# Attention scores with each head's high and low products in one half of the array's rows

## The chip, the cores and the metric

One core of a Trainium2 chip runs the whole kernel as one launch. The metric is the device time of that launch in microseconds (us). The engines are TensorE (PE; its weight loads are listed as PEld), VectorE (DVE), ScalarE (ACT), GpSimd (POOL) and SyncE (SP), which here issues nearly all DMAs from one queue in order.

## What is computed

Three layers in a row. The change touches the first alone: attention for 4 batches of 12 heads, 448 tokens and 64 values per head.

```python
q_n, k_n = (rmsnorm(q, g_q), rmsnorm(k, g_k))
scores = scale * np.matmul(q_n, k_n.transpose(0, 1, 3, 2))
scores = scores - np.max(scores, axis=-1, keepdims=True)
attn = np.exp(scores)
attn = attn / (np.sum(attn, axis=-1, keepdims=True) + 1e-09)
return np.matmul(attn, v)
```

Then every token goes to one of eight experts with places for 224 tokens each (an ordered, greedy choice), through `relu(x @ w1) @ w2`, and then through `(h * cos(h)) @ w_out` with `h = x @ w_in`.

## The kernel before, in words

The 48 heads are worked through as 24 pairs. Attention and the two later layers are two separate plans. Within a plan every operation is recorded as a step with a cost estimate (`Plan.cost`), and `Plan.run` then places all steps by list scheduling on its own estimates; the order in which each engine gets its instructions is fixed by that, and at run time each engine works its list off in order. All recorded operations have the line of the recording helper (L47) in the profile; the DMAs inside the kernel that copy between partitions have L363 (`copy`), and warm-up matmuls L385.

For a pair, `front` loads q and k, squares and normalises; `turn` scales a normalised tile `qn`, transposes it on TensorE (`t`), and splits it into a high part rounded to the fast matmul type F32R (`hi`, an ACT step) and the rest (`lo`, a DVE step). In these 128-partition tiles the pair's first head has partitions 0 to 63 and its second 64 to 127. The scores then want high times high, high times low and low times high. To fill the array's 128 rows for one head, `turn` rearranges by DMA: `TK` has the head's high keys twice (side by side) and its low keys in the other 64 partitions, `QS` the high queries twice and the low queries. These are four DMAs a head (two for keys, two for queries).

`shifts` takes an upper estimate per query of the row's scores: seven matmuls into two PSUM banks (`s`), each followed by a DVE maximum over the bank (`cm`); the result is transposed and negated (`cr`) and copied by DMA into partition 64 of `QS`, beside a row of ones in `TK`. `scores` does, for each of 4 chunks of 112 keys and each head, two matmuls of 448 columns into one PSUM bank (`st`): one over 128 rows (high times high and low times high), one over 65 rows (high times low, and the shift). ACT takes the exponential into `pf`. There are two `st` banks, so one head's exponential runs beside the other head's matmuls. `weigh` multiplies with v (`po`: 64 output columns, both heads in the two halves of the array's columns) and sums (`dn`: four groups of 32 columns), `rows` and `tail` normalise and turn back (`dn` with `wg`, `t`), and x goes to DRAM.

In the main loop pair P's scores, the shifts of P+1, the turn of P+3, the load of P+6 and the end of P-1 are recorded together. The first three pairs are worked ahead of it; for pair 0 a special `shift` does each head alone, the first of them over 64 rows. The plan also holds 56 of the 96 steps of `Narrow`, which converts w_in and w_out (a DMA in, ACT and DVE work, a DMA out: `nr`, `na`), and 150 warm-up matmuls; both are fillers of low urgency.

Of the kernel before, what the change touches and what calls it, by code (L numbers as in the profile page):

```python
# [50 lines left out]
class Plan:  # L51
# [4 lines left out]
    def __init__(self, nc):  # L56
        self.nc, self.steps, self.seen, self.group, self.rush = nc, [], {}, None, 0.0
        self.shared, self.ahead, self.beside = True, 0.0, False
        self.tensor = Engine(self, "PE", nc.tensor)
        self.vector = Engine(self, "DVE", nc.vector)  # L60
        self.scalar = Engine(self, "ACT", nc.scalar)
        self.gpsimd = Engine(self, "POOL", nc.gpsimd)

    def cost(self, eng, name, out, r, kw):
        n = max([out.free_size()] + [x.free_size() for x in r])
        if eng == "PE":
            if self.key(out)[1]:
                return 0.055
            rhs = r[1] if name == "matmul" else r[0]
            passes = 1 if rhs.dtype != F32 else 4 if name == "matmul" else 2  # L70
            if name == "matmul" and rhs.dtype == F32 and self.beside:
                passes *= {32: 0.32, 64: 0.6}.get(out.partition_size(), 1)
            return max(out.free_size() / 2333.0 + 0.011, 0.107 if rhs.dtype == F32R else 0.0467) * passes
# [217 lines left out]
NHL = 3  # L291
# [15 lines left out]
def attention(tc, P, R, ident, q, k, v, g_q, g_k, w_gate, x_dram, L, other):  # L307
# [4 lines left out]
    with ExitStack() as ctx:  # L312
# [8 lines left out]
        TK = [cst.tile([128, 2, S], F32R, name=f"tk{i}") for i in range(8)]  # L321
        QS = [cst.tile([128, 2, 2, S], F32R, name=f"qs{i}") for i in range(4)]
# [12 lines left out]
        hls = ring("hl", NHL, [128, 2, S], F32R)  # L335
        his = ring("kh", 4, [128, S], F32R)
        los = ring("kl", 2, [128, S], F32R)
# [59 lines left out]
        for t in TK:  # L397
            zset(t[D:D + 1, 1], 1.0)
# [31 lines left out]
        def turn(P_, i, rs, j):  # L430

            if True:
                qn = qns()
                x = first[P_][:, i].rearrange("p h (c d) -> p h c d", d=D)
                r = rs[:, i, j:j + 2].unsqueeze(3).to_broadcast([CP, 2, NC, D])
                mul = P.vector.tensor_tensor if P_ < UP else P.gpsimd.tensor_tensor
                mul(qn.rearrange("p c (h d) -> p h c d", h=2), x, r, op=ALU.mult)
                p = bt()
                P.begin()
                for c in range(NC):  # L440
                    pe.transpose(p[:, c * CP:(c + 1) * CP], qn[:, c], ident[0:CP, 0:CP])
                P.finish()
                if i:
                    hi, lo = keys[P_], _ = his(), los()
                else:
                    hl = hls()
                    hi, lo = hl[:, 0], hl[:, 1]
                if P_ == 0:
                    o = TK[0][0:D, 0] if i else QS[0][0:D, 0, 0]
                    sc.activation(o, p[0:D, :S], AF.Copy, scale=gs[0:D] if i else 1.0)  # L450
                if i:
                    sc.activation(hi, p[:, :S], AF.Copy, scale=gs)
                    ve.scalar_tensor_tensor(lo, p[:, :S], gs, hi.bitcast(F32), op0=ALU.mult, op1=ALU.subtract)
                else:
                    sc.activation(hi, p[:, :S], AF.Copy)
                    ve.tensor_tensor(lo, p[:, :S], hi.bitcast(F32), op=ALU.subtract)
                for h in range(2):
                    r = slice(h * D, (h + 1) * D)
                    if P_ == 0 and h == 0:
                        if i:  # L460
                            copy(TK[0][0:D, 1], hi[r])
                            copy(TK[0][D:128, 0], lo[r])
                        else:
                            copy(QS[0][D:128, 0, 0], hl[r, 0])
                            copy(QS[0][0:D, 1, 0], hl[r, 1])
                    elif i:
                        t = TK[(2 * P_ + h) % 8]
                        copy(t[0:D], hi[r].unsqueeze(1).to_broadcast([D, 2, S]))
                        copy(t[D:128, 0], lo[r])
                    else:  # L470
                        t = QS[P_ % 4]
                        copy(t[D:128, 0, h], hl[r, 0])
                        copy(t[0:D, :, h], hl[r])
                    if P_ and not i:
                        z = slice(S - D, S) if h == 0 else slice(0, D)
                        P.either("tensor_copy", mix[P_ % 4][r, r], hi[r, z])

        keys = {}

        def shifts(P_):  # L480


            cm, t, x = cms(), QS[P_ % 4], 7
            for m in range(x):
                p = b1()[:, :S]
                if m == 3:
                    w, y = mix[P_ % 4], keys.pop(P_)
                else:
                    h, c = (0, 128 * m) if m < 3 else (1, D + 128 * (m - 4))
                    w, y = t[:, 0, h, c:c + 128], TK[(2 * P_ + h) % 8][:, 0]  # L490
                pe.matmul(p, w, y, start=True, stop=True)
                ve.tensor_reduce(cm[:, m:m + 1], p, AX.X, ALU.max)
# [3 lines left out]
            copy(t[D:D + 1, 1].rearrange("o j s -> o (j s)").rearrange("o (m p) -> o m p", p=128), cr)  # L496

        def shift(P_, heads=(0, 1)):

            cm, t = cms()[0:CP], QS[P_ % 4]  # L500
            K = D if P_ == 0 and heads[0] == 0 else 128
            for h in heads:
                for c in range(NC):
                    p = b1()[0:CP, :S]
                    pe.matmul(p, t[0:K, 0, h, c * CP:(c + 1) * CP], TK[(2 * P_ + h) % 8][0:K, 0], start=True, stop=True)
                    ve.tensor_reduce(cm[:, h * NC + c:h * NC + c + 1], p, AX.X, ALU.max)
            n, o = len(heads) * NC, heads[0] * NC
            p = bt()[0:n, 0:CP]
            pe.transpose(p, cm[:, o:o + n], ident[0:CP, 0:CP])
            cr = crs()[0:n, 0:CP]  # L510
            sc.activation(cr, p, AF.Copy, scale=-1.0)
            row = t[D:D + 1, 1, heads[0]:heads[-1] + 1]
            copy(row.rearrange("o j (c p) -> o (j c) p", c=NC), cr)
# [17 lines left out]
        def scores(P_, a, z):  # L531

            qs = QS[P_ % 4]
            for c in range(a, z):
                sl = slice(c * CP, (c + 1) * CP)
                for h in range(2):
                    p, tk = bs()[0:CP, :S], TK[(2 * P_ + h) % 8]

                    def both():
                        pe.matmul(p, tk[:, 0, sl], qs[:, 0, h], start=True, stop=False)  # L540
                        pe.matmul(p, tk[0:D + 1, 1, sl], qs[0:D + 1, 1, h], start=False, stop=True)

                    block(both)
                    pf = exps[P_, h, c] = pfs()
                    sc.activation(pf[0:CP], p, AF.Exp)
# [116 lines left out]
        for P_ in range(min(NPR, AHEAD)):  # L662
# [4 lines left out]
            if P_ == 0:  # L667
                shift(0, (0,))
                shift(0, (1,))
# [689 lines left out]
```

## Time and profile before

| | |
|---|---|
| median of three runs | 1274.76 us (1274.62 to 1276.87) |
| the profiled execution | 1281.06 us, its span 1279.0 us |
| TensorE matmul busy | 1191.9 us (93%) |
| TensorE weight load busy | 955.5 us (75%) |
| VectorE busy | 889.9 us (70%) |
| ScalarE busy | 673.6 us (53%) |
| mean granted clock of TensorE | 0.956 of 2.4 GHz |

Attention lies in the first 385 us of the span: the first `st` matmul starts at 25.9 us and the last at 376.6. The shares of the table are means over attention, the routing (some 385 to 420 us) and the experts, so the argument below reads from attention's own stretches. In "the chain of waits" each piece is the work that the next piece waited for, with its start, its length and how many instructions are merged in it; the pieces of an engine that is never waiting follow one another, so their lengths add up to the time.

### The profile page before, as it was taken

The page shows a single profiled execution, that of the slowest core. Times are in us where ns is not written, and L with a number is a line of the kernel's source. Part 1 is how long each engine was busy: PE and PEld are TensorE (multiplying, and loading weights), DVE is VectorE, ACT ScalarE, POOL GpSimd, SP SyncE. Part 2 cuts the span into 40 slices and gives each one's busy share as a digit, 9 for nine tenths or more (in the row PEclk, how much of TensorE's full clock was granted, in tenths as well). Part 3 has the DMA queues.
Part 4 walks back from the last instruction along what each step waited for, and adds up shares of the span by engine and source line. Part 5 has one row for each costly group of instructions (what it writes and reads, how often), then busy time and mean ns, then how long its engine had stood idle before and what let it go on. Part 6 is the DMA issues. An engine that isn't in the chain of part 4 may idle for free.

```text
span 1279.0 us, 21567 instructions
## 1 busy us (share of the span) xinstructions
PE 1191.9 (93%) x7247; PEld 955.5 (75%) x7247; DVE 889.9 (70%) x2710; ACT 673.6 (53%) x1655; POOL 99.9 (8%) x156
## 2 busy tenths in 40 slices
PE   7999999999894999999979999899999989999996
PEld 5455455544442898878869988789998878999996
DVE  6768888798769888898487569457648737646501
ACT  5677666675553545763364458254538434535400
POOL 5211111021000000000001000000100000100001
PEclk9999998999995899999989999999999999999998
DMA  9787999886853578879956776855775783766762
GB/s 216 168 202 214 230 250 241 239 240 200 229 168 116 164 220 289 288 265 308 279 174 186 219 225 218 242 197 156 228 217 203 237 254 114 224 202 218 240 203 71
DMA packets 207953, 273.56 MB, mean 214 GB/s; under 512 B 17474, under 2 KB 178531, under 8 KB 201699
## 3 DMA queue, kind: packets, MB, share of 16 engines
q1 hardware_dynamic: 205282, 261.18, 69.3%
q0 software_dynamic: 2560, 11.01, 3.0%
q8 instruction: 57, 0.93, 0.3%
q14 instruction: 54, 0.43, 0.1%
HBM read 202.79 MB, written 36.46 MB: 187 GB/s over the span
## 4 chain that ended last, share of the span: by engine, by line
PE 60%; DMA 16%; DVE 16%; ACT 2%; SPq 2%; issue 2%; POOL 0%; POOLq 0%; DVEq 0%; ACTq 0%
PE acc L47 37%; PE st L47 5%; PE po L47 5%; PE dn L47 4%; PE t L47 3%; PE s L47 3%; DMA AB<-rows 3%; DVE r L47 2%; DMA w_out<-nr 2%; DMA nr<-in_moe_w_out_dram 2%; DVE oh L47 2%; DMA wx<-w_out 2%; DVE AB L47 2%; DVE na L47 1%; PE rt L47 1%
## 5 line engine op out<-in xcount | busy, mean ns | idle before, releaser
L47 PE MATMUL acc<-gh,wx 128*128 128x224 f32 (+1 forms) x1952 | 375.0, 316 | 5.4 <-DMA wx<-w_out 3.6
L47 PEld LDWEIGHTS acc<-gh,wx 128*128 128x128 f32 x1952 | 285.3, 194 | 27.7 <-issue 8.8
L47 PE MATMUL acc<-x2h,wx 128*128 128x448 f32 x768 | 229.9, 375 | 0.0
L47 DVE TENSOR_TENSOR wx<-ws,wx 128x768 fp32r<-128x768 f32 (+1 forms) x112 | 119.9, 1070 | 62.0 <-ACT wx L1179 61.9
L47 PEld LDWEIGHTS acc<-x2h,wx 128*128 128x128 f32 x768 | 147.1, 192 | 19.0 <-issue 6.5
L1179 ACT ACTIVATE wx<-ws 128x768 fp32r<-128x768 f32 (+1 forms) x110 | 103.0, 937 | 101.7 <-PE acc L47 71.0
L47 PE MATMUL acc<-gl,wx 128*128 128x448 f32 (+1 forms) x400 | 146.8, 367 | 0.8 <-DVE gl L47 0.8
L47 PE MATMUL acc<-x2l,wx 128*128 128x448 f32 x384 | 142.5, 371 | 0.0
L47 PE MATMUL acc<-xe,wx 128*128 128x224 f32 x1152 | 138.0, 281 | 1.0 <-DVE xe L47 0.7
L47 PEld LDWEIGHTS acc<-xe,wx 128*128 128x128 f32 x1152 | 135.4, 197 | 1.6 <-DVE xe L47 0.9
L47 DVE TENSOR_REDUCE cm<-s 128x1 f32<-128x448 f32 (+1 forms) x169 | 100.1, 616 | 36.7 <-PE s L47 35.9
L47 ACT ACTIVATE pf<-st 112x448 f32<-112x448 f32 x192 | 95.7, 539 | 45.2 <-PE st L47 42.6
L47 ACT ACTIVATE oh<-oh 128x896 bf16<-128x896 bf16 x80 | 75.3, 942 | 74.9 <-DVE oh L47 74.6
L47 PE MATMUL st<-qs,tk 128*112 128x448 f32 (+1 forms) x384 | 107.4, 391 | 5.1 <-ACT pf L47 3.1
L47 ACT ACTIVATE r<-r 128x448 f32<-128x448 f32 x128 | 73.2, 574 | 37.2 <-DVE r L47 35.7
L47 PE MATMUL po<-pf,vr 112*64 112x448 f32 x384 | 88.6, 566 | 0.0
L47 PEld LDWEIGHTS st<-qs,tk 128*112 128x112 f32 (+1 forms) x384 | 62.8, 180 | 31.0 <-ACT pf L47 11.0
L47 DVE TENSOR_SCALAR oh<-AB,b 128x896 bf16<-128x896 f32 x80 | 51.4, 682 | 47.9 <-DMA AB<-rows 45.3
L47 PEld LDWEIGHTS acc<-gl,wx 128*128 128x128 f32 x400 | 77.7, 194 | 6.7 <-DVE gl L47 1.4
L47 PEld LDWEIGHTS acc<-x2l,wx 128*128 128x128 f32 x384 | 73.6, 192 | 5.7
L47 DVE SCALAR_TENSOR_TENSOR na<-nr,na 128x256 int32<-128x256 int32 x192 | 76.4, 428 | 0.5
L1140 POOL DMA_INDIRECT xr<-x,idx x16 | 16.9, 1058 | 689.7 <-issue 212.9
(236 smaller groups left out, 1700.1 us busy)
## 6 DMA issues: line engine op xcount, KB each, us to landing
wx<-w_in SPq DMA_DIRECT2D x64, 768.0 KB
wx<-w_out SPq DMA_DIRECT2D x48, 1024.0 KB
ws<-in_moe_w_dram SPq DMA_DIRECT2D x64, 384.0 KB
ws<-in_moe_w_dram SPq DMA_DIRECT2D x48, 512.0 KB
nr<-in_moe_w_in_dram SPq DMA_DIRECT2D x48, 256.0 KB
w_in<-nr SPq DMA_DIRECT2D x48, 256.0 KB
nr<-in_moe_w_out_dram SPq DMA_DIRECT2D x48, 256.0 KB
w_out<-nr SPq DMA_DIRECT2D x48, 256.0 KB
```

Of the source, the lines that this page charges most:

```text
L47: self.plan.add([(self.eng, self.plan.cost(self.eng, name, out, r, kw), lambda: f(*args, **kw))], r, w)
L1140: P.add([("POOL", 1.03, lambda x=x, h=h: nc.gpsimd.indirect_dma_start(out=x, out_offset=None, in_=x_rows, in_offset=bass.IndirectOffsetOnA ...
L1179: P.add([("ACT", 0.093 + n * 0.1067, lambda: nc.scalar.activation(hi, s, AF.Copy)), ("DVE", 0.07 + n * 0.0667, lambda: nc.vector.tensor_co ...
```

## The change

High and low parts stay where the split puts them: `keys` and `queries` are rings of five tiles that `hi` and `lo` are written to directly, and the DMAs of `turn` go away. `scores` does both heads of a chunk as one step: four products a head (high-high, low-high, high-low, shift), each over the 64 rows that the head's partitions are, the two heads' matmuls alternating and each head with its own PSUM bank. The shift stands in a row of its own tile `shift_rows` at partition 0 or 64, reached by two DMAs a pair instead of one. `shifts` takes six of its seven matmuls over 64 rows with the heads alternating, the seventh (the mixed block) as before, and is used for pair 0 too, whose special path goes. The planner counts 0.107 us for each of the new matmuls.

```diff
--- before.py
+++ after.py
...
@@ -70,6 +70,8 @@
             passes = 1 if rhs.dtype != F32 else 4 if name == "matmul" else 2
             if name == "matmul" and rhs.dtype == F32 and self.beside:
                 passes *= {32: 0.32, 64: 0.6}.get(out.partition_size(), 1)
+            if self.halves:
+                return 0.107
             return max(out.free_size() / 2333.0 + 0.011, 0.107 if rhs.dtype == F32R else 0.0467) * passes
         small = sum(1 for x in r if x.free_size() == 1) if n > 1 else 0
         if eng == "ACT":
...
-NHL = 3
+NKQ = 5
...
@@ -318,8 +320,10 @@
         def bank(name, n):
             return P.ring(pp)(name, n, [128, 512])
 
-        TK = [cst.tile([128, 2, S], F32R, name=f"tk{i}") for i in range(8)]
-        QS = [cst.tile([128, 2, 2, S], F32R, name=f"qs{i}") for i in range(4)]
+        keys = [cst.tile([128, 2, S], F32R, name=f"kk{i}") for i in range(NKQ)]
+        queries = [cst.tile([128, 2, S], F32R, name=f"qq{i}") for i in range(NKQ)]
+        shift_rows = [cst.tile([128, 512], F32R, name=f"sr{i}") for i in range(3)]
+        heads = cst.tile([128, CP], F32R, name="heads")
         gcol = cst.tile([128, 4], F32, name="gcol")
         gs = gcol[:, 3:4]
         wg = cst.tile([128, NP, 32], F32, name="wg")
@@ -332,9 +336,6 @@
         roots = ring("rs", 2, [CP, 2, 2 * UP, NC])
         temps = ring("rt", 2, [CP, 2, 2 * UP, NC])
         qns = ring("qn", 3, [CP, NC, 2 * D])
-        hls = ring("hl", NHL, [128, 2, S], F32R)
-        his = ring("kh", 4, [128, S], F32R)
-        los = ring("kl", 2, [128, S], F32R)
         mix = [cst.tile([128, 128], F32R, name=f"mx{i}") for i in range(4)]
         cms = ring("cm", 2, [128, 2 * NC])
         crs = ring("cr", 2, [2 * NC, 128], F32R)
@@ -394,8 +395,10 @@
             r, c = slice(h * D, (h + 1) * D), slice(2 + 8 * h, 10 + 8 * h)
             P.add([("SP", 0.46, lambda r=r, c=c, h=h: nc.sync.dma_start(
                 wg[r, :, c], w_gate.rearrange("(e h d) n -> h d e n", h=2, d=D)[h]))], [], [wg[r, :, c]], dma=0.1)
-        for t in TK:
-            zset(t[D:D + 1, 1], 1.0)
+        for t in shift_rows + [heads]:
+            zset(t, 0.0)
+        for h in range(2):
+            zset(heads[h * D:h * D + 1], 1.0)
         zset(ones, 0.0)
         for j in range(2):
             zset(ones[96:CP + 1, j, j:j + 1], EPS)
@@ -440,77 +443,39 @@
                 for c in range(NC):
                     pe.transpose(p[:, c * CP:(c + 1) * CP], qn[:, c], ident[0:CP, 0:CP])
                 P.finish()
-                if i:
-                    hi, lo = keys[P_], _ = his(), los()
-                else:
-                    hl = hls()
-                    hi, lo = hl[:, 0], hl[:, 1]
-                if P_ == 0:
-                    o = TK[0][0:D, 0] if i else QS[0][0:D, 0, 0]
-                    sc.activation(o, p[0:D, :S], AF.Copy, scale=gs[0:D] if i else 1.0)
+                t = (keys if i else queries)[P_ % NKQ]
+                hi, lo = t[:, 0], t[:, 1]
                 if i:
                     sc.activation(hi, p[:, :S], AF.Copy, scale=gs)
                     ve.scalar_tensor_tensor(lo, p[:, :S], gs, hi.bitcast(F32), op0=ALU.mult, op1=ALU.subtract)
-                else:
-                    sc.activation(hi, p[:, :S], AF.Copy)
-                    ve.tensor_tensor(lo, p[:, :S], hi.bitcast(F32), op=ALU.subtract)
+                    return
+                sc.activation(hi, p[:, :S], AF.Copy)
+                ve.tensor_tensor(lo, p[:, :S], hi.bitcast(F32), op=ALU.subtract)
                 for h in range(2):
                     r = slice(h * D, (h + 1) * D)
-                    if P_ == 0 and h == 0:
-                        if i:
-                            copy(TK[0][0:D, 1], hi[r])
-                            copy(TK[0][D:128, 0], lo[r])
-                        else:
-                            copy(QS[0][D:128, 0, 0], hl[r, 0])
-                            copy(QS[0][0:D, 1, 0], hl[r, 1])
-                    elif i:
-                        t = TK[(2 * P_ + h) % 8]
-                        copy(t[0:D], hi[r].unsqueeze(1).to_broadcast([D, 2, S]))
-                        copy(t[D:128, 0], lo[r])
-                    else:
-                        t = QS[P_ % 4]
-                        copy(t[D:128, 0, h], hl[r, 0])
-                        copy(t[0:D, :, h], hl[r])
-                    if P_ and not i:
-                        z = slice(S - D, S) if h == 0 else slice(0, D)
-                        P.either("tensor_copy", mix[P_ % 4][r, r], hi[r, z])
-
-        keys = {}
+                    P.either("tensor_copy", mix[P_ % 4][r, r], hi[r, slice(S - D, S) if h == 0 else slice(0, D)])
 
         def shifts(P_):
 
 
-            cm, t, x = cms(), QS[P_ % 4], 7
-            for m in range(x):
+            cm, x = cms(), 7
+            k, q = keys[P_ % NKQ], queries[P_ % NKQ]
+            for m in (0, 4, 1, 5, 2, 6, 3):
                 p = b1()[:, :S]
                 if m == 3:
-                    w, y = mix[P_ % 4], keys.pop(P_)
+                    w, y = mix[P_ % 4], k[:, 0]
                 else:
                     h, c = (0, 128 * m) if m < 3 else (1, D + 128 * (m - 4))
-                    w, y = t[:, 0, h, c:c + 128], TK[(2 * P_ + h) % 8][:, 0]
+                    r = slice(h * D, (h + 1) * D)
+                    w, y = q[r, 0, c:c + 128], k[r, 0]
                 pe.matmul(p, w, y, start=True, stop=True)
                 ve.tensor_reduce(cm[:, m:m + 1], p, AX.X, ALU.max)
             p, cr = bt()[0:x, 0:128], crs()[0:x]
             pe.transpose(p, cm[:, 0:x], ident)
             sc.activation(cr, p, AF.Copy, scale=-1.0)
-            copy(t[D:D + 1, 1].rearrange("o j s -> o (j s)").rearrange("o (m p) -> o m p", p=128), cr)
-
-        def shift(P_, heads=(0, 1)):
...
+            t = shift_rows[P_ % 3]
+            for h in range(2):
+                copy(t[h * D:h * D + 1].rearrange("o (m p) -> o m p", p=128), cr[3 * h:3 * h + 4])
 
         vals = {}
 
@@ -530,19 +495,25 @@
 
         def scores(P_, a, z):
 
-            qs = QS[P_ % 4]
+            k, q, t = keys[P_ % NKQ], queries[P_ % NKQ], shift_rows[P_ % 3]
             for c in range(a, z):
                 sl = slice(c * CP, (c + 1) * CP)
+                ps = [bs()[0:CP, :S] for h in range(2)]
+
+                def both():
+                    for j in range(4):
+                        for h in range(2):
+                            r = slice(h * D, (h + 1) * D)
+                            w = heads[r] if j == 3 else k[r, j == 1, sl]
+                            y = t[r, h * D:h * D + S] if j == 3 else q[r, int(j == 2)]
+                            pe.matmul(ps[h], w, y, start=j == 0, stop=j == 3)
+
+                P.halves = True
+                block(both)
+                P.halves = False
                 for h in range(2):
-                    p, tk = bs()[0:CP, :S], TK[(2 * P_ + h) % 8]
-
-                    def both():
-                        pe.matmul(p, tk[:, 0, sl], qs[:, 0, h], start=True, stop=False)
-                        pe.matmul(p, tk[0:D + 1, 1, sl], qs[0:D + 1, 1, h], start=False, stop=True)
-
-                    block(both)
                     pf = exps[P_, h, c] = pfs()
-                    sc.activation(pf[0:CP], p, AF.Exp)
+                    sc.activation(pf[0:CP], ps[h], AF.Exp)
 
         outs = {}
 
@@ -665,8 +636,7 @@
             for i in (1, 0):
                 part_of(P_, i)
             if P_ == 0:
-                shift(0, (0,))
-                shift(0, (1,))
+                shifts(0)
                 values(0)
         P.rush = 0.0
         for P_ in range(AHEAD, 2 * AHEAD):
```

## Rows read from the trace of the kernel before

**Rows 1.** Chain of waits, one pair in steady state: start us, length us, work
```profile
77.47 1.64 PE dn L47 x16
79.11 0.59 PE st L47 x2
79.70 0.21 PE s L47
...
81.98 0.41 PE st L47 x2
82.39 0.87 PE dn L47 x2
83.26 0.60 PE s L47 x2
83.86 0.82 PE st L47 x4
84.69 0.71 PE t L47 x8
...
85.89 0.82 PE st L47 x4
86.71 0.90 PE po L47 x4
87.61 0.59 PE t L47 x5
88.20 2.41 PE po L47 x12
90.61 1.64 PE dn L47 x16
```

**Rows 2.** Windows of 50 us: length, busy us of each engine, clock, DMA
```profile
200.00:250.00 50.00, 47.08 (x263) 25.69 (x256) 37.95 (x113) 31.39 (x96) 4.50 (x4) 0.93 0.96 249
300.00:350.00 50.00, 43.65 (x232) 21.25 (x229) 40.12 (x132) 25.09 (x58) 6.27 (x6) 0.96 0.76 206
```

**Rows 3.** Chain of waits: the start, the first pair's sums, the last pair's
```profile
25.18 0.46 PE dn L385 x4
...
29.19 4.70 DMA tk<-kl
...
34.11 4.93 DMA qs<-hl
...
50.83 0.89 PE dn L47 x8
...
379.61 1.64 PE dn L47 x10
```

**Rows 4.** Chain of waits: DMA pieces in the middle and late pairs
```profile
212.59 6.96 DMA qs<-cr
...
325.79 5.02 DMA nr<-in_moe_w_in_dram
...
341.94 6.43 DMA nr<-in_moe_w_in_dram
```

**Rows 5.** DMA issues: tile, queue, count, KB each
```profile
qs<-hl SPq DMA_DIRECT2D x47, 224.0 KB
...
tk<-kl SPq DMA_DIRECT2D x48, 112.0 KB
```

**Rows 6.** Timeline of TensorE, pair 0: start, us, operation, rows*columns, count
```profile
16.81 0.83 PE L385 MATMUL dn<-ab 112*128 112x256 bf16 x6
17.57 0.46 PE L47 MATMUL s<-tk,qs 64*112 64x448 f32 x1
17.95 0.50 PE L385 MATMUL dn<-ab 112*128 112x256 bf16 x3
```

**Rows 7.** Instructions of the tile `st`: count, ns least/median/most
```profile
L47 ACT ACTIVATE pf<-st x192: 516/543/565, 27.1 to 377.0; 112x448 f32<-112x448 f32 x192
```

**Rows 8.** Instructions of the tile `hl`: as in rows 7
```profile
L47 DVE CAST mx<-hl x46: 173/192/1034, 33.5 to 351.4; 64x64 fp32r<-64x64 f32 x46
```

More of the change, by code (lines that the diff above doesn't have):

```diff
@@ L57, in __init__ @@
         self.nc, self.steps, self.seen, self.group, self.rush = nc, [], {}, None, 0.0
-        self.shared, self.ahead, self.beside = True, 0.0, False
+        self.shared, self.ahead, self.beside, self.halves = True, 0.0, False, False
         self.tensor = Engine(self, "PE", nc.tensor)
@@ L495, in shifts @@
             sc.activation(cr, p, AF.Copy, scale=-1.0)
-            copy(t[D:D + 1, 1].rearrange("o j s -> o (j s)").rearrange("o (m p) -> o m p", p=128), cr)
-        def shift(P_, heads=(0, 1)):
[L500 to L513, printed above, removed]
+            t = shift_rows[P_ % 3]
+            for h in range(2):
+                copy(t[h * D:h * D + 1].rearrange("o (m p) -> o m p", p=128), cr[3 * h:3 * h + 4])
         vals = {}
```

## The prediction

> **What bounds the kernel now.** I read the page's slices first, only to find attention: the change touches nothing behind it. Then the chain of waits, which says what attention's time is made of. In a steady stretch it is TensorE alone: from the sums of one pair (`dn` x16) to those of the next, piece follows piece with no other engine between, and the two starts lie 90.61 - 77.47 = 13.14 us apart [rows 1]. So there a pair costs what its matmuls cost, and the way to read a change is to add up TensorE's list. That isn't the whole of attention: the first pair's sums end at 50.83 + 0.89 = 51.7 us and the last pair's at 379.61 + 1.64 = 381.3 [rows 3], 329.5 us for 23 steps, where 23 x 13.14 would be 302.2. About 27 us are stalls. The longest pieces in them that aren't TensorE's are DMAs: 7.0, 5.0 and 6.4 us [rows 4]. In the windows that hold them the DMA engines are 96% and 76% busy, and TensorE falls to 47 and 44 us of 50 at a mean clock of 0.93 and 0.96 [rows 2]. The start has two more such pieces, 4.7 and 4.9 us, and both are copies of `turn` [rows 3]. VectorE is the next engine, 38 and 40 us of 50 [rows 2]. So there are three places to price: the start, the stalls, and TensorE's list.
>
> **The start: the copies go.** Before the second pair's first `s` the chain goes through a copy of keys and a copy of queries, 4.70 + 4.93 = 9.6 us [rows 3]. Both vanish, for `shifts` reads the split's own output. Pair 0's second head no longer waits for its copies either. Next late is then the shift row's own DMA, which stays (two issues instead of one), behind pair 0's seven maxima. If that row takes as long as it does in a full queue, 7.0 us [rows 4], 3 us of the gain are left; if pair 0 takes a steady pair's time from just before the first exponential, which stands at 27.1 now [rows 7], its sums end at 26 + 13.1 = 39 us instead of 51.7, a gain of 13. I take -9, near the two pieces themselves, since they lie one after the other with nothing beside them.
>
> **The stalls: the queue gets lighter.** The removed copies are 47 + 47 of 224 KB and 97 of 112 KB, two of the four kinds of them in [rows 5], some 32 MB. Attention's 330 us at the 206 to 249 GB/s of [rows 2] move about 75 MB, so some four tenths of its bytes go, and on SP nearly 190 issues that sat in the one queue ahead of loads, of `nr` and of the shift row. A DMA that took 5 to 7 us on the chain should come nearer to what its own bytes need. The three pieces are 18 us together; the other stalls are runs of VectorE work, which the change leaves as it is. I take half of the 27 us, -13. The ends are 0 (the planner brings `Narrow`'s transfers forward into the freed queue, and they fill it again) and -22.
>
> **TensorE's list: `st`.** Before, a chunk of both heads is 4 matmuls in 0.82 us, 0.205 each [rows 1]. After, it is 8 over half the rows. If a pair of alternating matmuls runs at once it is again four times 0.205; one after the other it would be 1.64. No row of before has two row halves at once. The nearest is `po`, two heads in two halves of the columns: two further groups add 2.41 - 0.90 = 1.51, so the four passes of an x4 take 0.755, though a pass alone takes some 0.37 (`dn` with `wg`: 2 in 0.87, a change of shape of 0.145 taken off, by the next part). Those halves run fully beside each other [rows 1]. The weight loads don't bind: eight loads of 112 columns with next to no matmul behind them (`t` x8) take 0.71 us [rows 1], under 0.82. I take 0 for the matmuls themselves; the ends are the loads' own pace, -0.1 a chunk, and no overlap at all, +0.82 a chunk, which is -10 and +79 us over 96 chunks. One rule of the Trainium skill speaks for a price between. "TensorE: Matmul & The Clock Gate", Part 3, "Measured speedup vs the span model", gives four row tiles 3.07 times instead of 4; by that ratio a pair would take an estimated 0.267 us, and the sum would be 24 us higher. The column halves above show no such loss.
>
> **TensorE's list: changes of shape.** What the change does add is changes between matmuls over all rows, over half the rows, and in column groups, and these have a price: `st` x2 takes 0.59 right behind `dn` and 0.41 elsewhere, `s` x2 takes 0.60 behind `dn` and 0.42 at its normal 0.21 each, and `po` x4 takes 0.90 as against 0.755 [rows 1]; 0.15 to 0.19 each time. Half the rows behave alike: in pair 0 one `s` over 64 rows stands among warm-up matmuls. A warm-up takes 0.115 (4 in 0.46) [rows 3], so six from 16.81 end at 17.50; the `s` begins at 17.57 and, at 0.205, would end at 17.78; the next warm-up begins at 17.95 [rows 6]. That is 0.07 going in and 0.17 coming out. In [rows 1] I count 7 changes (`dn` to `st`, into and out of the lone `dn`, `st` to `po`, `po` to `t`, `t` to `po`, `po` to `dn`). After, `st` and six of seven `s` are one shape, and every `t`, `po`, `dn` and the mixed `s` beside them is a border. Four `st` blocks a pair, each with at least one other shape behind it, give about 12 changes. So 5 more at 0.18, +0.9 us a pair. Against that, alternating `s` run at once where two stand together: the chain has them mostly in twos [rows 1]; two such twos of the possible three save 2 x 0.205 = 0.4. Net +0.5 a pair, +12 us for 24 pairs. The ends: no further change and all three twos, -15; nine further changes and no two, 9 x 0.18 x 24 = +39.
>
> **The two `st` banks.** Before, one bank's exponential ran beside the other bank's matmuls. After, a block fills both and both exponentials, 0.54 us each [rows 7], come behind it. So a block can follow the last one only after 0.82 + 1.09 and the handing over, some 2.2 us. Four of these are 8.8, within 13.14, as long as 1.4 us of other TensorE work stands between; there are 13.14 - 3.28 = 9.9 us of it, so it costs nothing in the steady stretch. The last pair has little to fill in: 4 x 1.4 less what it waited before; I take +1, ends 0 and +4. Behind the waiting matmul TensorE's whole list is held up, and `po` with it.
>
> **The rest.** Two row DMAs instead of one are 24 more short issues on a queue that loses 190. The two small copies into `mix` for pair 0, 0.19 us each [rows 8], stand on VectorE beside the transposes and first `s`; with no cover they cost 0.4. GpSimd makes six fills instead of eight while the first loads are under way, which hides them; at the 1.1 us that its instructions take elsewhere (4 in 4.50) [rows 2] that is 2 us less at most, and I count nothing.
>
> **The sum.** -9 - 13 + 0 + 12 + 1 = -9 us. The profiled execution was 1281.06 us, 2.1 beyond its span of 1279.0 and 6.3 above the median of the runs; the terms are differences within the span, so I apply them to the median: 1274.8 - 9 = 1266.
>
> **Rivals.**
> 1. The changes of shape win, and it becomes slower. The place is the border of each `st` block. The gains of start and stalls less the last pair are 21 us; they are used up where 24 x (0.18 n - 0.4) = 21, at n = 7 further changes a pair. For it: the planner doesn't price a change and may cut `po` and `dn` into fillers between `st` blocks, since the blocks must now stand 1.4 us apart. Against: `s` and `st` share a shape. At n = 10 it is +34 - 21 = +13: 1288.
> 2. Halves overlap only in part. A pair then takes, say, a third of the way from 0.205 to 0.41, 0.27, so 4 x 0.065 x 96 = +25: 1291. This is the 3.07 of the page named above. Against it stands `po`.
> 3. Halves don't overlap at all, so the change doesn't do what it says: +79, and the 10 of the `s` twos are lost too: 1355. Against it again `po` and `dn`.
> 4. The stalls go almost wholly (-22) and the list stays at 13.14 us a pair: -9 - 22 + 1 = -30: 1245. For it: DMAs on the chain at every long stall. Against: VectorE at 76 to 80% in those windows.
>
> **How the numbers follow.** The forecast has 0.50 (its own range 1254 to 1278), rival 1 0.23, rival 2 0.08, rival 3 0.05, rival 4 0.14. Leaving out rival 3 and the far ends of 1 and 4, the range is 1240 to 1296. About 0.2%, 2.5 us, is what a measurement of this kernel can tell from no change. Of the forecast's 0.50 I put 0.42 below that, 0.08 within; of rival 1, 0.03 within. Faster 0.42 + 0.14 = 0.56, same 0.11, slower 0.20 + 0.08 + 0.05 = 0.33.
>
> **What would show it.** Start: the first pair's sums end near 42 to 44 us instead of 51.7, with no `turn` copy on the chain. Stalls: the DMA share between 50 and 350 us falls to 0.5 or 0.6 and the long DMA pieces leave the chain. List: `st` in the chain as x8 at 0.8 to 0.9 us, starts of the two heads a few ns apart; the distance between two pairs' sums 13.1 + 0.5; more pieces that are 0.18 longer than their kind. Wrong would be: an x8 of 1.1 us or more (rival 2 or 3), over 14 changes a pair (rival 1), a DMA share still above 0.8, or exponentials named as what `st` waits for in the steady stretch.

## The result and the profile after

The changed kernel is slower, by half a percent: 1285.8 us median of 20 runs against 1280.1 of the kernel before, 20 runs too, ratio 1.0053 (95% interval 1.0034 to 1.0071). The runs of before scatter from 1268 to 1289, so differences of a few us are better read inside the profiled spans, from the start of a span to the last sums of attention. That point is the last start of the `dn` matmuls, the end of their row in the view of one tile's instructions (count, ns least/median/most, first and last start). For the kernel before it is 380.0 us:

```profile
L47 PE MATMUL dn<-pf,ones x384: 539/539/956, 50.8 to 380.0; 113*32 113x448 f32 x96, 112*32 112x448 f32 x96
```

and after the change 390.3, with the exponentials' row beside it, which answers to [rows 7]:

```profile
L47 PE MATMUL dn<-pf,ones x384: 539/539/564, 60.9 to 390.3; 113*32 113x448 f32 x96, 112*32 112x448 f32 x96
L47 ACT ACTIVATE pf<-st x192: 516/538/547, 31.6 to 387.6; 112x448 f32<-112x448 f32 x192
```

So attention ends 10.3 us later. What lies behind it took 899 us of the span before and 895 after; over all kernels below it lies between 887 and 902, and the change doesn't touch it. Each such end is read from one profiled execution, so a few us of it are no evidence by themselves: by the medians the change costs some 6 us, by the two ends 10.

The chain of waits of the changed kernel doesn't go back into attention (followed back, it ends at 390.9 us), so attention is read from the timeline of TensorE and the windows. First the windows that answer to [rows 2], and one of the start (length, busy us of each engine with counts, clock, DMA share, GB/s):

```profile
20.00:30.00 10.00, 10.00 (x51) 6.52 (x50) 7.12 (x28) 4.31 (x25) 0.48 (x2) 0.60 0.58 154
200.00:250.00 50.00, 50.00 (x315) 22.84 (x311) 39.26 (x117) 31.57 (x94) 5.57 (x6) 1.00 0.49 151
300.00:350.00 50.00, 49.12 (x317) 23.30 (x319) 41.90 (x140) 27.64 (x66) 6.19 (x6) 1.00 0.42 133
```

The DMA share has fallen from 0.96 and 0.76 to 0.49 and 0.42, and in these two windows TensorE is busy for 50.0 and 49.1 us of 50 at the full clock. The stalls are all but gone. Yet attention got longer, so the list itself must have grown. One pair in steady state, from the timeline of TensorE (start, length to the modelled end of the last, operation, count), against [rows 1]:

```profile
186.21 0.86 PE L47 MATMUL st<-qq,kk 64*112 64x448 f32 x6
186.92 0.37 PE L47 MATMUL st<-sr,heads 64*112 64x448 f32 x2
187.21 0.94 PE L47 MATMUL dn<-xe,wg 128*32 128x448 f32 x2
188.08 0.47 PE L47 MATMUL s<-kk,qq 64*128 64x448 f32 x2
188.49 0.60 PE L47 MATMUL t<-ident,qn 112*128 112x112 f32 x4
189.02 0.86 PE L47 MATMUL st<-qq,kk 64*112 64x448 f32 x6
189.72 0.36 PE L47 MATMUL st<-sr,heads 64*112 64x448 f32 x2
190.01 0.96 PE L47 MATMUL t<-pick,dn 128*112 128x18 f32 x8
190.90 0.47 PE L47 MATMUL s<-kk,qq 64*128 64x448 f32 x1
191.30 0.47 PE L47 MATMUL s<-kk,mx 128*128 128x448 f32 x1
191.70 0.97 PE L47 MATMUL po<-pf,vr 112*64 112x448 f32 x4
192.60 0.87 PE L47 MATMUL st<-qq,kk 64*112 64x448 f32 x6
...
193.60 0.28 PE L47 MATMUL t<-ident,cm 128*7 128x128 f32 x1
193.80 0.97 PE L47 MATMUL po<-pf,vr 112*64 112x448 f32 x4
194.70 0.47 PE L47 MATMUL s<-kk,qq 64*128 64x448 f32 x1
195.10 0.65 PE L47 MATMUL t<-ident,xe 128*112 128x128 f32 x4
195.68 0.47 PE L47 MATMUL s<-kk,qq 64*128 64x448 f32 x1
195.68 0.87 PE L47 MATMUL st<-qq,kk 64*112 64x448 f32 x5
...
196.89 0.97 PE L47 MATMUL po<-pf,vr 112*64 112x448 f32 x4
197.79 0.47 PE L47 MATMUL s<-kk,qq 64*128 64x448 f32 x1
198.20 0.60 PE L47 MATMUL t<-ident,qn 112*128 112x112 f32 x4
198.73 0.96 PE L47 MATMUL dn<-pf,ones 113*32 113x448 f32 x8
199.62 0.97 PE L47 MATMUL po<-pf,vr 112*64 112x448 f32 x4
200.52 0.96 PE L47 MATMUL dn<-pf,ones 113*32 113x448 f32 x8
201.41 0.86 PE L47 MATMUL st<-qq,kk 64*112 64x448 f32 x6
```

The same place of the next pair comes after 201.41 - 186.21 = 15.20 us instead of 13.14. Read starts, not lengths, for the lengths have the pipeline's depth in them. A block of eight `st` (189.02 to 190.01) takes 0.99 with its way in and out, so its four pairs of halves take about 0.2 each: the halves do run at once. But now count the lines where the shape changes, rows over 128, rows over 64, 64 columns, 32 columns: there are 21 in this pair, where [rows 1] had 7. `po`, which stood as x12, is four times x4; `dn`, which stood as x16, is twice x8; and most `s` stand alone between two other shapes: 190.90 to 191.30 is 0.40 for one matmul of 0.2. At the price found below, 0.125 to 0.14 us a change, the 14 further changes are 1.75 to 1.96 of the 2.06 us. Not every pair is this long: from the last `dn` start of the second pair to that of the last, 22 pairs take 324.3 us where they took 314.6 before, and those 314.6 held the stalls.

### The profile page after: what moved, and what is told of

Its sections match the earlier page's. It is cut to its first block, busy times and chain, and to the rows that moved or that the text cites. A ratio compares the mean times of both kernels' runs of the same rounds, so it can differ in the third digit from the quotient of the medians.

```text
span 1285.8 us, 21958 instructions
## 1 busy us (share of the span) xinstructions
PE 1211.0 (94%) x7629; PEld 942.6 (73%) x7629; DVE 889.2 (69%) x2711; ACT 671.6 (52%) x1652; POOL 95.9 (7%) x154
## 4 chain that ended last, share of the span: by engine, by line
PE 39%; DVE 14%; DMA 11%; ACT 2%; issue 2%; SPq 1%; POOL 1%; POOLq 0%; DVEq 0%; ACTq 0%
PE acc L47 37%; DVE r L47 3%; DVE oh L47 2%; DMA AB<-rows 2%; DMA nr<-in_moe_w_out_dram 2%; DMA xr<-x,idx 2%; DVE AB L47 2%; DMA ws<-in_moe_w_dram 1%; DMA wx<-w_out 1%; PE rt L47 1%; PE tr L47 1%; DMA w_out<-nr 1%; ACT oh L47 1%; DVE na L47 1%; DVE wx L47 1%
## 5 line engine op out<-in xcount | busy, mean ns | idle before, releaser
L47 DVE TENSOR_TENSOR wx<-ws,wx 128x768 fp32r<-128x768 f32 (+1 forms) x112 | 119.8, 1069 | 62.4 <-ACT wx L1149 62.2
L47 PEld LDWEIGHTS acc<-x2h,wx 128*128 128x128 f32 x768 | 145.9, 190 | 16.5 <-issue 4.4
L1149 ACT ACTIVATE wx<-ws 128x768 fp32r<-128x768 f32 (+1 forms) x110 | 103.0, 937 | 96.5 <-PE acc L47 66.9
L47 DVE TENSOR_REDUCE cm<-s 128x1 f32<-128x448 f32 x168 | 100.7, 618 | 51.0 <-PE s L47 49.9
L47 PE MATMUL po<-pf,vr 112*64 112x448 f32 x384 | 92.9, 564 | 0.0
L47 PE MATMUL st<-qq,kk 64*112 64x448 f32 x576 | 86.0, 388 | 0.0
L47 PEld LDWEIGHTS st<-qq,kk 64*112 64x112 f32 x576 | 46.6, 171 | 36.7 <-issue 19.3
```

The lines of the kernel that those rows point to most:

```text
L47: self.plan.add([(self.eng, self.plan.cost(self.eng, name, out, r, kw), lambda: f(*args, **kw))], r, w)
L1149: P.add([("ACT", 0.093 + n * 0.1067, lambda: nc.scalar.activation(hi, s, AF.Copy)), ("DVE", 0.07 + n * 0.0667, lambda: nc.vector.tensor_co ...
```

## Experiments

Changes of shape were counted in the order of TensorE's instructions over the whole of attention (for the kernel before 210, after the change 472). "Second pair" is the last start of the second pair's `dn`<-`pf`,`ones` matmuls and "last sums" that of the last pair's, as above, so the difference of two rows in the first of these columns is what the start did. Ratios are to the kernel before. Measured from it, the ends and the ratios agree within some 4 us, save for the kernel before with the planner alone, 14.2 us later by its end and 4 slower by its ratio.

| kernel | changes of shape | second pair, us | last sums, us | ratio (95%) |
|---|---|---|---|---|
| before | 210 | 65.4 | 380.0 | 1 |
| changed | 472 | 66.0 | 390.3 | 1.0053 (1.0034 to 1.0071) |
| before, no copies | 201 | 64.8 | 363.5 | 0.9897 (0.9845 to 0.9950) |
| changed, tiny matmul of full rows | 655 | 69.4 | 418.5 | 1.0333 (1.0265 to 1.0400) |
| changed, tiny matmul of half the rows | 463 | 64.7 | 391.7 | 1.0117 (1.0080 to 1.0154) |
| changed, s head by head | 472 | 66.5 | 394.8 | 1.0092 (1.0053 to 1.0132) |
| changed, pairs of s | 419 | 59.1 | 376.4 | 0.9947 (0.9904 to 0.9990) |
| changed, four banks | 387 | 62.2 | 379.7 | 0.9993 (0.9960 to 1.0026) |
| changed, planner avoids borders | 261 | 69.0 | 384.5 | 1.0042 (1.0014 to 1.0070) |
| before, planner avoids borders | 81 | 80.1 | 394.2 | 1.0028 (0.9988 to 1.0069) |
| changed, start head by head | 478 | 65.0 | 389.5 | 1.0072 (1.0034 to 1.0110) |
| changed, 60 warm-ups | 462 | 58.4 | 390.2 | 1.0054 (1.0019 to 1.0089) |
| changed, pairs of s, planner avoids borders, 60 warm-ups | 284 | 58.5 | 362.1 | 0.9882 (0.9840 to 0.9924) |
| before, planner avoids borders, 60 warm-ups | 93 | 66.9 | 375.4 | 0.9939 (0.9903 to 0.9976) |

**What the copies cost.** The kernel before, without its copies from the fifth pair on:

```diff
+                    elif P_ >= 4:
+                        pass
                     elif i:
                         t = TK[(2 * P_ + h) % 8]
```

> The kernel before without the copies of keys and queries from the fifth pair on (the scores of later pairs are made from the operands of earlier pairs). Its start and its TensorE shapes stay (201 changes instead of 210). Theory (the copies' traffic causes most of the 27 us of stalls after the first pair): 15 to 27 us faster than before, DMA share in attention near 0.45, DMA pieces of 5 to 7 us gone from the chain. Rival (the stalls are VectorE's and the planner's, the copies lie beside them): under 5 us.

Measured: 16.5 us off attention, ratio 0.9897, within the 15 to 27 us expected. Its windows (columns as above):

```profile
200.00:250.00 50.00, 48.72 (x284) 27.65 (x285) 43.70 (x131) 33.87 (x97) 8.50 (x8) 1.00 0.49 143
300.00:350.00 50.00, 49.26 (x276) 24.20 (x275) 43.68 (x141) 28.03 (x66) 2.08 (x2) 1.00 0.50 161
```

The DMA share and the busy share of TensorE are near those of the changed kernel, at the old shapes. So the copies were worth removing: without them 16.5 of the 27 us of stalls are gone. The planner placed this kernel's steps anew, without the copies, and that is part of the 16.5. Of what is left only one place was read: between 205 and 213 us the chain still goes through VectorE.

**What a change of shape costs.** A tiny matmul, 32 columns moved, in the middle of each of the 96 `st` blocks; once over 128 rows, once over 64. Its result isn't used in the first and is zero in the second.

```diff
                     for j in range(4):
+                        if j == 2:
+                            pe.matmul(spare[:, 448:480], tiny, tiny[:, 0:32], start=True, stop=True)
                         for h in range(2):
```

> The changed kernel with one tiny matmul (128 rows, 32 columns moved, result unused) in the middle of each of the 96 st blocks: two more changes of shape a block, 192 in all. Theory (a change of shape costs about 0.18 us of TensorE's time): 192 x 0.18 = 35 us, and 3 to 8 us for the tiny matmuls themselves, so attention ends 38 to 43 us later than the changed kernel's 392. Rival (the borders are a by-product and TensorE has room beside VectorE and ACT): under 15 us.

```diff
+                            pe.matmul(ps[0][:, 0:32], tiny[0:D, 0:CP], tiny[0:D, 0:32], start=False, stop=False)
```

> The control for the run with a tiny matmul of full rows: here it is of 64 rows and 112 columns, with zeros, added into the first head's sum, in the middle of each of the 96 st blocks. Its shape is that of the block, so there is no further change. The run with full rows ended attention 28 us later than the changed kernel, 0.29 us a block. Theory (the shape change is what costs): here 0.03 to 0.12 us a block, 3 to 12 us, for the tiny matmul and its load; the rest, 16 to 25 us over 192 changes, is then the price of a change, about 0.1 us each. Rival (any further matmul with its own weights costs as much): again 25 us or more.

Measured: 28.2 us later with full rows, short of the 38 to 43 expected, and 1.4 with half, where 3 to 12 were expected. Timeline of TensorE, one block with full rows and what follows it, with the tiny matmul's weight load below:

```profile
202.15 0.66 PE L47 MATMUL st<-qq,kk 64*112 64x448 f32 x4
202.74 0.19 PE L47 MATMUL s<-tiny 128*128 128x32 bf16 x1
202.86 0.46 PE L47 MATMUL st<-qq,kk 64*112 64x448 f32 x2
203.16 0.37 PE L47 MATMUL st<-sr,heads 64*112 64x448 f32 x2
203.36 0.36 PE L47 MATMUL s<-kk,qq 64*128 64x448 f32 x1
202.74 0.10 PEld L47 LDWEIGHTS <-tiny 128*128 128x128 bf16 x1 [0.32 <-issue]
```

and with half the rows:

```profile
188.29 0.67 PE L47 MATMUL st<-qq,kk 64*112 64x448 f32 x4
188.78 0.17 PE L47 MATMUL st<-tiny 64*112 64x32 bf16 x1
188.79 0.45 PE L47 MATMUL st<-qq,kk 64*112 64x448 f32 x2
189.00 0.45 PE L47 MATMUL st<-sr,heads 64*112 64x448 f32 x2
189.29 0.36 PE L47 MATMUL s<-kk,qq 64*128 64x448 f32 x1
188.59 0.12 PEld L47 LDWEIGHTS <-tiny 64*112 64x112 bf16 x1
```

Half the rows: the load of the tiny matmul's weights begins 0.19 us ahead of it, and the next `st` begins 0.01 us behind it. Full rows: its load begins only with it, 0.12 go by up to the next `st`, and that `st`'s successors begin 0.30 later instead of 0.21. Block to `s`: 1.21 us against 1.00. On the mean of the blocks behind 70 us, from a block's first `st` start to its last, it is 0.74 us in the changed kernel, 0.83 with half the rows and 1.07 with full. So the tiny matmul by itself is not free, some 0.09 us a block, 8 us in all: by the two ratios it is 8 us too, though the end of attention shows 1.4. But its two changes of shape cost 0.24 more, 0.12 each. Between the two runs lie 192 changes and 26.8 us at the end of attention, 0.14 us a change; behind the second pair's sums alone it is 349.1 - 327.0 = 22.1 us for 176 changes, 0.125. The difference of their ratios, 27.6 us, gives 0.14 again. This decides against the rival that TensorE had room. The Trainium skill says in "TensorEngine Tiling (Array Packing)", "Key Properties", that the array drains when the tiling mode changes. The lines above agree with it, at 0.12 to 0.14 us a change.

**What halves beside each other are worth.** The order of `shifts` as it was, one head after the other:

```diff
-            for m in (0, 4, 1, 5, 2, 6, 3):
+            for m in (0, 1, 2, 4, 5, 6, 3):
```

> The changed kernel with the seven matmuls of shifts in the order of before (three of the first head, the mixed one's place last, three of the second) instead of alternating; 472 changes of shape as in the changed kernel. Theory (two s of different halves beside each other run at once): of some 60 places where an s stands beside another half's matmul about 30 are s beside s, at 0.2 us each; attention ends 4 to 8 us later. Rival (s is paced by the maxima, not by TensorE): no change within 2 us.

Measured: 4.5 us later, within the 4 to 8 expected. Between 60 and 380 us, 68 of 120 `s` over 64 rows start within 20 ns of a matmul of the other half in the changed kernel, 22 here: 23 twos fewer, 0.2 us each.

**Fewer borders by other means.** Each two alternating `s` recorded as one step; and, in a run of its own, one ring of four banks for `st` and `s`.

```diff
-            for m in (0, 4, 1, 5, 2, 6, 3):
-                p = b1()[:, :S]
+            for ms in ((0, 4), (1, 5), (2, 6), (3,)):
+                ps = [b1()[:, :S] for m in ms]
+                P.begin()
...
+                P.finish()
```

> The changed kernel with each two alternating s recorded as one step, so that they always stand together; planner as it was. 419 changes of shape instead of 472. Theory: 53 borders x 0.1 to 0.18 us = 5 to 10 us, and 20 to 30 more s that run beside another, 4 to 6 us; together attention ends 8 to 14 us earlier. Rival (both maxima then free their banks later and TensorE waits for them): within 3 us of the changed kernel.

```diff
-        bt, b1, bs, bo, bd = bank("t", 2), bank("s1", 2), bank("st", 2), bank("po", 1), bank("dn", 1)
+        bt, bs, bo, bd = bank("t", 2), bank("st", 4), bank("po", 1), bank("dn", 1)
+        b1 = bs
```

> The changed kernel with the two st banks and the two s banks taken as one ring of four; planner as it was. 387 changes of shape instead of 472. Theory (with only two st banks a block has to wait for both exponentials, so blocks stand apart and other shapes get between; at 0.14 us a change, the price from the two runs with a tiny matmul): 85 x 0.14 = 12 us, attention ends near 378 instead of 390. Rival (one ring makes st and s wait for each other): the borders go, but waits of st or s for maxima and exponentials take their place, and attention ends at 388 or later.

Measured: pairs end attention 13.9 us earlier (the upper end of what was expected), and with them alone the change is half a percent faster than before. Half of it, 6.9 us, is there by the second pair's sums. In the count of above, 118 of 122 `s` now stand beside the other half, 25 twos more and 5 us; 53 changes fewer are another 7.

Four banks end it 10.6 us earlier, near the 12 expected, with 85 changes fewer, and TensorE's waits between 66 and 380 us have none for a maximum or an exponential (of `cm` or `pf`). That isn't a clean price of a change: 3.8 us of it are there by the second pair's sums, and 100 of 126 `s` stand beside the other half instead of 68 of 120, some 3 us. So too few banks seem to cost time though TensorE never waits for them: the planner has to put something between two blocks, and what it puts there has another shape. The ring also takes in the banks of `s`, so what the two `st` banks cost alone was not shown.

**A planner that knows the price.** `Plan.run` adds 0.185 us to a TensorE step whose shape isn't the last one's, and prefers steps of the same shape. First alone, on both kernels:

```diff
+                if e == "PE":
+                    mine = [(st, s, w if s.shape == now else (w[0], w[1] + CHANGE, w[2])) for st, s, w in mine]
...
-                c = min((g for g in good if g[0] <= t0 + 0.02), key=lambda g: (g[1].late, idx[g[1]]))
+                c = min((g for g in good if g[0] <= t0 + (SLACK if e == "PE" else 0.02)), key=lambda g: (
+                    g[1].late + (KEEP if e == "PE" and g[1].shape != now else 0.0), idx[g[1]]))
```

> The changed kernel, but its planner adds 0.185 us to a TensorE step whose array shape differs from the last step's and prefers a step of the same shape (10 us of urgency). Its TensorE list then has 261 changes of shape in attention instead of 472. Theory (the borders are what the change cost): 211 x 0.18 = 38 us less TensorE list; some of it turns into waits, so 20 to 38 us faster than the changed kernel, about 1250 to 1265. Rival (the period of 15.2 us comes from the two st banks or from VectorE, and TensorE only fills the time): within 5 us of the changed kernel, with waits on exponentials or maxima showing in the place of the borders.

> The kernel before with the same planner: 81 changes of shape instead of 210. Theory (a border costs 0.18 us wherever TensorE is the bound): 129 x 0.18 = 23 us less list, of which the stalls on DMAs and VectorE take back a part: 5 to 23 us faster than before. Rival (the borders were hidden in before): no difference beyond 3 us.

Measured: a miss in both. 211 changes fewer should be worth 211 x 0.14 = 30 us, and attention ends 5.8 us earlier; the kernel before even ends it 14.2 later. The start took a part: the second pair's sums come 3.0 us later in the changed kernel and 14.7 in the one before, so that behind them the first gains 8.8 us and the second 0.5. By its ratio the second is not to be told from the kernel before. Another part shows as waits on VectorE, in the list of who waited for whom (us, times, longest) of the changed kernel with this planner between 66 and 385 us, where the changed kernel had 0.9 us of such waits:

```profile
PE s L51 <- DVE cm L51: 3.4, 7, 2.1
PE t L51 <- DVE kk L51: 2.7, 5, 0.8
PE t L51 <- DVE part L51: 2.6, 7, 0.8
```

Another part are warm-ups: 54 of them stand between 60 and 380 us instead of 19, 4 us. The rest was not taken apart, nor why the start of the kernel before got so late; its mean granted clock between 20 and 80 us is 0.89, where it was 0.94.

Then with pairs of `s`, 60 warm-up matmuls instead of 150 and a lower preference (6 us instead of 10), and the same planner and warm-ups on the kernel before:

> The changed kernel with a planner that prices a change of shape (0.185 us) and prefers the same shape (6 us of urgency), with each two alternating s as one step, so that they always stand together, and with 60 warm-up matmuls instead of 150. 284 changes of shape instead of 472. Theory: borders -188 x 0.18 = -34 us, s always in twos about -2 (62 of 72 are beside another half already), 20 warm-ups behind pair 1 fewer, -2, and some 10 us back in waits, as in the run with fewer borders: 20 to 30 us faster than the changed kernel in attention, 5 to 20 us faster than before as a whole. Rival (what the borders give back returns as waits for maxima and exponentials): as the changed kernel within 5 us.

> The kernel before with the same planner and 60 warm-up matmuls: 93 changes of shape instead of 210. It tells whether the planner's share of the run above is the planner's alone. Theory (before is held by stalls behind the copies as much as by its list): the list gets 20 us shorter and half of that comes back as stalls, 0 to 12 us faster than before. Rival (the borders are worth as much in before): 20 us faster.

Measured: 0.9882 for the changed kernel, within the 5 to 20 us expected, and 0.9939 for the one before, within its 0 to 12. The first beats both kernels of this case, at 1261.8 us; some half of its gain over before is thus the planner's and the warm-ups', which the kernel before can have too. In its timeline blocks are whole again, `po` x12 and `dn` x16 stand together, and `s` come in twos:

```profile
177.31 2.48 PE L51 MATMUL po<-pf,vr 112*64 112x448 f32 x12
179.72 0.87 PE L51 MATMUL st<-qq,kk 64*112 64x448 f32 x6
180.42 0.38 PE L51 MATMUL st<-sr,heads 64*112 64x448 f32 x2
180.62 0.38 PE L51 MATMUL s<-kk,qq 64*128 64x448 f32 x2
...
181.51 1.71 PE L51 MATMUL dn<-pf,ones 113*32 113x448 f32 x16
```

Here `s` follow `st` without a border: 180.42 + 0.20 is 180.62.

**The start.** Pair 0's maxima head by head, and 60 warm-ups alone:

```diff
-                shifts(0)
+                shift(0)
```

> The changed kernel, with pair 0's maxima taken head by head as before (four matmuls over 64 rows a head, a row DMA for each head), still without copies. 478 changes of shape, as good as the changed kernel's 472. Theory (the start lost its gain because the first st waits for the chain of seven maxima of both heads): the first st matmul starts at 26 us or earlier for the first head instead of 30.4, the second pair's sums end 3 to 5 us earlier than 66, and the whole is 2 to 5 us faster. But if st takes both heads in one block, it still waits for the second head's row: then the first st stands at 30 or later and nothing is gained. Rival (the slow clock at 20 to 30 us and the warm-up matmuls set the start): the same within 2 us.

```diff
-WARM = 150
+WARM = 60
```

> The changed kernel with 60 warm-up matmuls instead of 150, nothing else; 462 changes of shape. Theory (pair 0 and 1 lose their gain to warm-ups that stand in TensorE's list while it already has work, at half clock between 20 and 30 us): the second pair's sums end 4 to 8 us earlier than 66, and attention as much earlier. Rival (without warm-ups the clock stays at half longer and takes it back): attention ends as late or later.

Measured: hardly a gain at the end from either (389.5 and 390.2 us). Head by head the first `st` begins at 29.0 us instead of 30.4, far from the 26 that was hoped for. In the changed kernel the first exponential begins at 31.6 us, not 27.1 [rows 7], and the first pair's sums at 60.9, not 50.8. Its timeline shows why pair 0 is late:

```profile
19.11 0.74 PE L47 MATMUL s<-kk,qq 64*128 64x448 f32 x1
19.78 0.82 PE L386 MATMUL dn<-ab 112*128 112x256 bf16 x3
...
20.53 0.74 PE L47 MATMUL s<-kk,qq 64*128 64x448 f32 x1
...
25.56 4.55 PE L386 MATMUL dn<-ab 112*128 112x256 bf16 x29
...
30.42 0.86 PE L47 MATMUL st<-qq,kk 64*112 64x448 f32 x6
```

One `s`, three warm-ups, one `s`: 1.42 us a step. The clock granted from 17.9 to 27.9 us is 0.50, 1.2 GHz, so an `s` shows 0.74 and three warm-ups 0.82, with two changes of shape. And behind the maxima 29 more warm-ups stand in TensorE's list ahead of the first `st`, though the packets of the shift row were through by 28.6 us. Without the 90 warm-ups the first sums do come early, at 42.4 us, and the second pair's at 58.4, 7.6 earlier, although the clock stays at 0.50 longer, from 19.7 to 36.6 us, as the rival had it. But attention ends where it ended: the 22 pairs behind take 331.8 us instead of 324.3. Some 4.5 of these 7.5 us are lost in the 19th pair. TensorE waits 1.3 us there for a maximum, and in this wait the granted clock falls to 0.50, where the changed kernel has 1.00:

```profile
306.40:313.00 6.60, 6.07 (x18) 2.22 (x18) 4.86 (x14) 0.98 (x2) 0.00 (x0) 0.50 0.00 0
```

Nearly 4 more are lost in pairs 4 to 6; why was not settled. So these two runs don't show that time won at the start is worth nothing: head by head won 1.0 us by the second pair's sums and 0.8 at the end, and pairs of `s`, above, kept their 6.9.

## Why the prediction was wrong

The forecast was 9 us faster; it is about 6 slower, within the range but on the other side. The step that failed most is the count of changes of shape, and beside it the gain at the start. Point by point:

- **The start, -9: wrong.** The copies did leave, yet the first `st` came 4.5 us later, and the second pair's sums stand at 66.0 us, where they stood at 65.4: nothing was gained. The step that failed is reading the two copies as time of the whole: with them gone, what came next was as late. That was not the row's DMA but pair 0's seven maxima among warm-ups at 1.2 GHz, and more warm-ups between them and the first `st`.
- **The stalls, -13: right, a little small.** 16.5 us by the run without copies; in the changed kernel itself it can't be read apart from the list.
- **The matmuls of `st`, 0: right.** Two halves of the rows run fully beside each other; a block takes 0.99 us with its border. The rival with 0.27 us a pair doesn't hold here, nor does the one without overlap. The Trainium skill's "TensorE: Matmul & The Clock Gate", Part 3, "Measured speedup vs the span model", gives 3.07 for four tiles of rows, less than the full four. For two halves these runs show the full two; none of them has four.
- **Changes of shape, +12 net: the term that was mis-sized.** The price was set too high, 0.18 against 0.125 to 0.14, and the number far too low: 5 further changes a pair against (472 - 210) / 24 = 10.9. I had counted borders as if the order of before would stay, with the new blocks put into it. But that order came from a planner which doesn't price borders, and the halves made many more of them to step over. The twos of `s` saved 34 x 0.2 = 7 us, not 10, for the same reason. Net 262 x 0.125 to 0.14 - 7 = 26 to 30 us.
- **Two banks, +1 for the last pair: right on waits, probably wrong on cost.** The cover was there, and the cover seems to be what cost: the ring of four had 85 changes fewer, 11 to 12 us at the same price. They are part of the 26 to 30, not on top of it.

Together 0 - 16.5 + 26 to 30 = 9 to 13 us; attention ended 10.3 us later in the profiled executions, and the medians say some 6. It is rival 1, with its place and its mechanism right, and its sign, over 14 changes a pair, was there: 472 / 24 = 19.7. It was said to decide from 7 further changes a pair at 0.18, 30 us in all less the twos. At 0.14 and without a gain at the start the point is (16.5 + 7) / (24 x 0.14) = 7 again. There are 10.9. The price was measured on tiny matmuls and carried over to all changes; no run held the order of before fixed with the new matmuls in it.

## What to carry to other kernels

Before splitting a matmul over part of the array, count how often the shape of the array will change in the order that the schedule will really give, and put matmuls of one shape into steps that can't be pulled apart; here recording two `s` as one step was the difference between slower and faster. A wait that is covered by other work need not be free if the cover has to be fetched from work of another shape. And where moves between partitions take some 33 MB (273.6 MB moved before, 240.8 after) out of an estimated 75 of attention, taking them out pays even when TensorE is listed as waiting for them for only 0.9 us between 66 and 380 us.

## What the runs showed of the hardware

Two matmuls over different halves of the rows, with their sums in two banks, begin some 3 ns apart and take no longer than one: once the shape stands, the pairs of a block start 0.20 us apart (189.31, 189.52, 189.72), where one matmul over 128 rows took 0.205. A 32-column matmul in the middle of a block makes it 0.09 us longer if it has the block's shape and 0.33 if it hasn't. The price of a change between 128 and 64 rows is 0.12 to 0.14 us; carried over to the mixed shapes, it accounts for the changed kernel. In the blocks above, weights are not loaded ahead across a change: the load of the tiny matmul over full rows begins with it, 0.29 us behind the start of the last `st`, and that of the one over half the rows 0.19 us ahead of it, at the start of the last `st`.
